# Tail-query scores as concurrent 64-row matmuls, with transposes and sums in one PSUM tile and smaller last output pieces

## The chip, the cores and the metric

The kernel runs on one core of a Trainium2 chip. The metric is the device time of one execution in microseconds (us). TensorE appears as PE in the profile, VectorE as DVE, ScalarE as ACT, GpSimd as POOL and SyncE as SP. The "granted clock" is the share of full TensorE clock that the throttle granted.

The spread of a single kernel is often 1% here. So two versions are compared only from runs of the same rounds on the same chip.

## The reference, cut to what matters

Attention with a relative position bias for 8 batches and 8 heads, then a bilinear feed-forward block on the result.

```python
# q, k, v: (8, 8, 576, 64); bias_table: (32, 8)
scores = q @ k.transpose(0, 1, 3, 2) / 8 + bias_table[bucket].transpose(2, 0, 1)[None]
attn = softmax(scores)                     # rows of 576 keys
x = (attn @ v).transpose(0, 2, 1, 3).reshape(4608, 512)
out = ((x @ w_a) * (x @ w_b)) @ w_out      # w_a, w_b: 512x1536, w_out: 1536x512
```

## The kernel before

Two heads form a head pair; there are 32 pairs, `p`, four to a batch. A sequence of 576 is cut into 512 "main" positions (four tiles of 128) and a "tail" of 64. Scores are made transposed, with keys on the partitions, so that the exponentials can be used as weights for `attn @ v`. The bias is a multiplication by `exp(bias)` after the exponential.

The schedule is written by hand. Stage `s` makes the scores of pair `s`, finishes pair `s-1` (its sums `av`, the normalisation into `XG`, the transposition into `xn`), and fills TensorE with units of the feed-forward block. A stage has two "score groups" (`qk(s, 0)` and `qk(s, 2)`). The first four pairs run in a denser prologue, and pairs 0 to 7 transpose Q and K on TensorE. From pair 8 on Q and K come transposed by DMA.

```python
ps_sc = ...tile_pool(name="ps_sc", bufs=2, space=PSUM)   # 2 tiles of 2 banks
ps_av = ...tile_pool(name="ps_av", bufs=1, space=PSUM)   # 1 bank: warm-up, av sums
ps_tr = ...tile_pool(name="ps_tr", bufs=1, space=PSUM)   # 1 bank: transposes
ps_ff = ...tile_pool(name="ps_ff", bufs=2, space=PSUM)   # 2 tiles of 1 bank
# ... (cut)
trb = ps_tr.tile([128, 1024], BF16, tag="tr", name="trb")

def tr_half():                       # the two halves of trb in turn
    turn[0] ^= 1
    return trb[:, 512 * turn[0]:512 * turn[0] + 512]

def qk(p, t0):                       # scores of main queries and main keys
    qT, kT, _ = operands(p)
    for t in (t0, t0 + 1):
        ps = ps_sc.tile([128, 2, 512], FP32, tag="sc", name=f"qk{p}_{t}")
        for hh in range(2):          # head hh lives on rows 64*hh..64*hh+63
            r = slice(64 * hh, 64 * hh + 64)
            nc.tensor.matmul(out=ps[:, hh, :], lhsT=kT[r, t, :], rhs=qT[r, :, :], ...)

def qk_tail(p):
    qT, kT, z = operands(p)          # z: both tails, block-diagonal (zeros elsewhere)
    ps = ps_sc.tile([128, 2, 512], FP32, tag="sc", name=f"qkt{p}")
    for t in range(NM):              # tail queries on main keys: 128 rows, 128 columns
        nc.tensor.matmul(out=ps[:, 0, :]...[:, :, t, :], lhsT=kT[:, t, :], rhs=z[:, 0, :], ...)
    # tail keys on main queries (512 columns), then on tail queries (2 x 64 columns)
    # ... (cut)

def mul_tail(p):                     # both multiplications by exp(bias) of a tail
    # ... (cut)
    nc.vector.tensor_tensor(out=x, in0=x, in1=e, op=MULT)                 # 128x512
    nc.vector.tensor_tensor(out=at[:, o:o + 192], ..., op=MULT)

def av(p, jqs, pool=None, tag="av"):
    pav = (pool or ps_av).tile([128, 3, 2, Dh + 1], FP32, tag=tag, ...)
    # ... (cut) matmuls into pav, then on DVE a reciprocal and a multiply for each
    # group, from pav into XG

def t_x(p, jqs=range(5), eng=None):  # XG -> xn
    if 4 <= p < NP - 1:
        nc.sync.dma_start_transpose(...)     # two transposing DMAs
        return
    ps = tr_half()                           # pairs 0-3 and 31: on TensorE
    # ... (cut) transposes, then a copy by ACT or DVE

def ff_o_last(c, tt, half):          # the last 128 rows of the output
    cs = slice(256 * half, 256 * half + 256)
    # ... (cut) 12 matmuls of 256 columns into po
    ob = wrk.tile([128, DM], FP32, tag="ob", ...)
    nc.scalar.activation(out=ob[:, 0:128], in_=po[:, 0:128], func=ACTF.Copy)
    nc.vector.tensor_copy(out=ob[:, 128:256], in_=po[:, 128:256])
    for hh, eng in enumerate((nc.sync, nc.scalar)):
        eng.dma_start(out=out[r0:r0 + ST, cs], in_=ob[64 * hh:64 * hh + 64, 0:256])

# prologue (cut to its middle)
av(1, h0, ps_ff, "ffn")
# ...
t_x(0, h0)
sc(1, 1)
av(2, h0)
mul_tail(0)
tail0(1)
t_x(1, h0)
# ...
# a stage; U stands for feed-forward units, A(...) for av of pair s-1
head = [U, ex(s, 1), A(0, 1, 2), U, mul(s, 0), t_q(s + 1), U, mul(s, 1)]
late = [A(3, 4), U, t_x(s - 1)]
pair = [v_next(s), (qk(s, 2), ex(s, 2)), U, ex(s, 3), t_k(s + 1, ACT), U, mul(s, 2)]
tail = [(qk_tail(s), ex_tail(s)), U, U, mul_tail(s)]
```

The softmax here doesn't subtract the row's maximum and nothing guards it: scores larger than these inputs give would overflow.

Of the kernel before, what the change touches and what calls it, by code (L numbers as in the profile page):

```python
# [13 lines left out]
def kernel(  # L14
# [35 lines left out]
    ps_sc = ctx.enter_context(tc.tile_pool(name="ps_sc", bufs=2, space=bass.MemoryType.PSUM))  # L50
    ps_av = ctx.enter_context(tc.tile_pool(name="ps_av", bufs=1, space=bass.MemoryType.PSUM))
    ps_tr = ctx.enter_context(tc.tile_pool(name="ps_tr", bufs=1, space=bass.MemoryType.PSUM))
    ps_ff = ctx.enter_context(tc.tile_pool(name="ps_ff", bufs=2, space=bass.MemoryType.PSUM))
# [57 lines left out]
    wo_sb = wpool.tile([128, NDF, DM], BF16, name="wo")  # L111
    xn_sb = [wpool.tile([128, NT], BF16, name=f"xn{mc}") for mc in range(NMC)]
    g_sb = [wpool.tile([128, DM], BF16, name=f"g{df}") for df in range(NDF)]

# [66 lines left out]
    def padding():  # L181
# [5 lines left out]
        for i in range(2):  # L187
# [14 lines left out]
                            op=mybir.AluOpType.subtract)  # L202
    warm = ps_av.tile([128, 512], FP32, tag="av", name="warm")

    def warm_up(n):
        for _ in range(n):
            nc.tensor.matmul(out=warm[:, :], lhsT=zero_sb[:, 0:128], rhs=zero_sb[:, :],
                             start=True, stop=True)
# [39 lines left out]

    trb = ps_tr.tile([128, 1024], BF16, tag="tr", name="trb")
    turn = [0]  # L250
# [70 lines left out]


    def qk(p, t0):
        qT, kT, _ = operands(p)
        st[p].setdefault("at", [None] * NM)
        for t in (t0, t0 + 1):
            ps = ps_sc.tile([128, 2, 512], FP32, tag="sc", name=f"qk{p}_{t}")
            for hh in range(2):
                r = slice(64 * hh, 64 * hh + 64)
                nc.tensor.matmul(out=ps[:, hh, :], lhsT=kT[r, t, :], rhs=qT[r, :, :],  # L330
                                 start=True, stop=True)
            st[p]["ps", t] = ps

    def ex(p, t):
# [45 lines left out]
    def qk_tail(p):  # L380
        qT, kT, z = operands(p)
        ps = ps_sc.tile([128, 2, 512], FP32, tag="sc", name=f"qkt{p}")
        for t in range(NM):
            nc.tensor.matmul(  # L384
                out=ps[:, 0, :].rearrange("p (h t c) -> p h t c", h=2, t=NM)[:, :, t, :],
                lhsT=kT[:, t, :], rhs=z[:, 0, :], start=True, stop=True)
# [13 lines left out]
    def ex_tail(p):  # L400
        ps, pt = st[p]["ps"]
        n = main_tail(p)
        at = att[p % 2]
        m = 512 + n
        if n < SM:
            m += ST
        else:
            nc.scalar.activation(out=at[:, m:m + ST], in_=pt, func=ACTF.Exp, scale=scale)
        nc.scalar.activation(out=at[:, 0:m], in_=ps[:, :, :].rearrange("p a x -> p (a x)")[:, 0:m],  # L409
                             func=ACTF.Exp, scale=scale)  # L410
        st[p]["att"] = at

    def mul_tail(p):
        at, w, wt = st[p]["att"], W_sb[p % 4], Wt_sb[:, p % 4, :]
        x = at[:, 0:512].rearrange("p (h t c) -> p h t c", h=2, t=NM)
# [3 lines left out]
        nc.vector.tensor_tensor(out=x, in0=x, in1=e, op=MULT)  # L419
        o = 512 + main_tail(p) - 128  # L420
        nc.vector.tensor_tensor(out=at[:, o:o + 192], in0=at[:, o:o + 192], in1=wt[:, 191::-1], op=MULT)

# [18 lines left out]
    def av(p, jqs, pool=None, tag="av"):  # L441
# [3 lines left out]
        rc = wrk.tile([128, 3, 2], FP32, tag="rc", name=f"rc{p}_{jqs[0]}")  # L445
        pav = (pool or ps_av).tile([128, 3, 2, Dh + 1], FP32, tag=tag, name=f"av{p}_{jqs[0]}")
        for slot, jq in enumerate(jqs):
# [64 lines left out]

    def ff_o_last(c, tt, half):
        cs = slice(256 * half, 256 * half + 256)
        po = ff_bank(f"po{c}_{tt}_{half}")
        for df in range(NDF):
            nc.tensor.matmul(out=po[:, 0:256], lhsT=g_sb[df][:, 128 * tt:128 * tt + 128],
                             rhs=wo_sb[:, df, cs], start=(df == 0), stop=(df == NDF - 1))
        ob = wrk.tile([128, DM], FP32, tag="ob", name=f"ob{c}_{tt}_{half}")
        nc.scalar.activation(out=ob[:, 0:128], in_=po[:, 0:128], func=ACTF.Copy)  # L520
        nc.vector.tensor_copy(out=ob[:, 128:256], in_=po[:, 128:256])
        for hh, eng in enumerate((nc.sync, nc.scalar)):
            r0 = S * (2 * tt + hh) + SM
            eng.dma_start(out=out[r0:r0 + ST, cs], in_=ob[64 * hh:64 * hh + 64, 0:256])

# [20 lines left out]
    for c in range(NCH):  # L546
# [8 lines left out]
        for tt in range(4):  # L555
            if c == NCH - 1 and tt == 3:
                units += [lambda c=c, tt=tt, half=half: ff_o_last(c, tt, half) for half in range(2)]
                continue
# [143 lines left out]
    for s in range(4, NP + 1):  # L702
# [12 lines left out]
        elif new:  # L715
            head = [U, lambda: ex(s, 1), A(0, 1, 2), U, lambda: mul(s, 0), lambda: t_q(s + 1), U,
                    lambda: mul(s, 1)]
            late = [A(3, 4), U, lambda: t_x(s - 1)]
            pair = [lambda: v_next(s), lambda: (qk(s, 2), ex(s, 2)), U, lambda: ex(s, 3),
                    lambda: t_k(s + 1, ACT), U, lambda: mul(s, 2)]  # L720
            tail = [lambda: (qk_tail(s), ex_tail(s)), U, U, lambda: mul_tail(s)]
# [63 lines left out]
```

## Time and profile before

| | before |
|---|---|
| median of 4 runs | 425.33 us (425.02 to 425.51) |
| span in the profile | 423.6 us |
| PE busy | 407.6 us, 96% |
| mean granted clock | 0.988 |

From the page of the kernel before: busy time of each engine with its share of the span (PE's line), then the busy tenths and the granted clock in 40 equal slices of the span, then the chain of work that ended last, by engine.

```profile
PE 407.6 (96%) x3471; PEld 207.6 (49%) x3471; DVE 239.0 (56%) x562; ACT 245.6 (58%) x347; POOL 130.7 (31%) x187
...
PE   7689899999999999999999999999999999999995
...
PEclk9689999999999999999999999999999999999999
...
PE 85%; DMA 7%; POOL 3%; DVE 2%; ACT 1%; issue 1%; ACTq 0%; DVEq 0%; POOLq 0%
```

PE is the bottleneck in nearly every slice. The exceptions are slices 1, 2, 3 and 5 (within the first 53 us) and the last one. So in the middle only matmul time counts, and at the two ends waits count.

The timeline of PE of the kernel before, in the prologue. Columns: start, duration, engine, line, operation, tiles (out<-in), row and column form, shape; a bracket gives idle time ahead and what ended it.

```profile
24.94 0.23 PE L448 MATMUL av<-vt,atk 128*128 128x130 bf16 x1
...
26.26 0.27 PE L480 MATMUL trb<-ident,XG 128*128 128x128 bf16 x2
26.37 0.22 PE L448 MATMUL av<-vt,atk 128*128 128x130 bf16 x1
...
28.37 0.27 PE L480 MATMUL trb<-ident,XG 128*128 128x128 bf16 x2
...
30.46 0.27 PE L480 MATMUL trb<-ident,XG 128*128 128x128 bf16 x2 [0.99 <-DVE xn L260]
...
31.33 0.22 PE L448 MATMUL av<-vt,att 128*128 128x130 bf16 x1
...
35.10 0.23 PE L448 MATMUL av<-vt,att 128*128 128x130 bf16 x1
...
36.06 0.33 PE L480 MATMUL trb<-ident,XG 128*128 128x128 bf16 x3
```

Transposes (into `trb`) and sums (into `av`) follow one another almost without idle time. They lie in different tiles. The one wait shown, at 30.46, is of transposes for a copy out of their own tile `trb`.

The waits of PE from 20 to 100 us, kernel before: waiting line, what it waited for, total us, times, longest. Then the busy times of the engines from 24 to 50 us (PE, PEld, DVE, ACT, POOL, then granted clock, DMA share, GB/s).

```profile
PE trb L480 <- DVE xn L260: 1.0, 1, 1.0
PE pa L498 <- DMA kn<-in_k_dram: 0.9, 1, 0.9
...
PE av L448 <- DVE XG L462: 0.2, 1, 0.2
```

```profile
24.00:50.00 26.00, 23.27 (x329) 16.64 (x326) 21.52 (x66) 18.33 (x29) 14.31 (x20) 0.99 1.39 189
```

A tail in the steady part, from PE's timeline of the kernel before: four matmuls of tail queries on main keys, one of 512 columns, two of 64. It lasts from 210.89 to 211.39 (the start of the next matmul), that is 0.50 us. The last two lines are feed-forward matmuls.

```profile
210.89 0.39 PE L384 MATMUL qkt<-ZB,KB 128*128 128x128 bf16 x4
211.12 0.38 PE L388 MATMUL qkt<-QB,ZB 128*128 128x512 bf16 x1
211.33 0.22 PE L392 MATMUL trb<-ZB 128*128 128x64 bf16 x2
...
244.79 1.03 PE L498 MATMUL pa<-xn,wa 128*128 128x512 bf16 x4
245.65 1.03 PE L508 MATMUL pb<-xn,wb 128*128 128x512 bf16 x4
```

The end, from the timeline of all engines of the kernel before. The last matmul ends at 418.65.

```profile
419.70 0.28 ACT L520 ACTIVATE ob<-po 128x128 f32<-128x128 f32 x1 [1.49 <-DMA out_dram<-ob]
420.01 0.29 DVE L521 COPY ob<-po 128x128 f32<-128x128 f32 x1 [1.47 <-ACT ob L520]
420.34 0.50 ACTq L524 DMA_DIRECT2D out_dram<-ob  x1
```

The last copy of ACT waits for an older output DMA out of the same buffer, then DVE's copy waits for ACT's, then come issue and landing.

### The profile page before, as it was taken

What the parts mean: (1) busy time and instruction counts of PE and PEld (TensorE: products, weight loads), DVE (VectorE), ACT (ScalarE), POOL (GpSimd) and SP (SyncE); (2) the same over time, 40 slices, a digit from 0 to 9 for tenths busy, and PEclk for the clock granted to TensorE, in tenths of its full rate; (3) what the DMA queues carried; (4) which work ended last, traced back from release to release, by engine and by line L of the source; (5) the groups of instructions that cost most, each with busy time, mean ns of one, the idle gap of its engine ahead of it and who ended that gap; (6) DMA issues with size and microseconds to landing.
All of it is one profiled execution on the core that took longest, in us unless ns stands there. A gap on an engine that the chain in (4) does not pass through costs nothing.

```text
span 423.6 us, 8798 instructions
## 1 busy us (share of the span) xinstructions
PE 407.6 (96%) x3471; PEld 207.6 (49%) x3471; DVE 239.0 (56%) x562; ACT 245.6 (58%) x347; POOL 130.7 (31%) x187
## 2 busy tenths in 40 slices
PE   7689899999999999999999999999999999999995
PEld 3367545535555444555454544454545455444443
DVE  5788568546654776467646665476547662431320
ACT  4676676566665766576657674866566742322321
POOL 9654458596008700690039201500000000000000
PEclk9689999999999999999999999999999999999999
DMA  9999999999439970999099905950430012002004
GB/s 117 200 201 171 204 144 187 140 185 130 82 73 148 124 106 19 151 159 119 16 128 158 139 15 115 143 90 17 88 91 15 15 39 76 1 2 99 0 8 94
DMA packets 139756, 42.46 MB, mean 100 GB/s; under 512 B 115994, under 2 KB 135226, under 8 KB 139714
## 3 DMA queue, kind: packets, MB, share of 16 engines
q0 software_dynamic: 81264, 18.89, 57.5%
q1 hardware_dynamic: 53010, 13.67, 20.4%
q10 hardware_dynamic: 5440, 9.34, 7.1%
q8 instruction: 27, 0.44, 0.5%
q14 instruction: 15, 0.12, 0.1%
HBM read 39.18 MB, written 9.45 MB: 115 GB/s over the span
## 4 chain that ended last, share of the span: by engine, by line
PE 85%; DMA 7%; POOL 3%; DVE 2%; ACT 1%; issue 1%; ACTq 0%; DVEq 0%; POOLq 0%
PE pb L508 22%; PE pa L498 22%; PE po L531 21%; PE av L452 9%; PE qk L330 7%; DMA kn<-in_k_dram 4%; PE av L448 2%; DMA wb<-in_moe_w_b_dram 2%; PE qkt L384 1%; PE qkt L388 1%; POOL qn L121 1%; POOL vt L159 1%; POOL kn L121 1%; POOL tl L153 1%; DMA out_dram<-ob 1%
## 5 line engine op out<-in xcount | busy, mean ns | idle before, releaser
L337 ACT ACTIVATE at<-qk 128x1024 bf16<-128x1024 f32 x112 | 111.5, 1024 | 29.1 <-PE qk L330 11.1
L511 DVE TENSOR_TENSOR g<-pb,ha 128x512 bf16<-128x512 f32 (+1 forms) x112 | 75.1, 671 | 79.4 <-PE pb L508 61.5
L498 PE MATMUL pa<-xn,wa 128*128 128x512 bf16 (+1 forms) x448 | 112.1, 372 | 1.8 <-DMA kn<-in_k_dram 0.9
L508 PE MATMUL pb<-xn,wb 128*128 128x512 bf16 (+1 forms) x448 | 111.8, 372 | 0.1
L502 ACT ACTIVATE ha<-pa 128x512 f32<-128x512 f32 (+1 forms) x112 | 65.2, 582 | 73.5 <-PE pa L498 73.5
L531 PE MATMUL po<-wo,g 128*128 128x512 bf16 x420 | 99.1, 379 | 0.0
L342 DVE TENSOR_TENSOR at<-at,W 128x1024 bf16<-128x1024 bf16 x112 | 75.0, 684 | 20.5 <-ACT at L337 20.5
L498 PEld LDWEIGHTS <-wa 128*128 128x128 bf16 x448 | 40.2, 98 | 48.0 <-issue 8.3
L508 PEld LDWEIGHTS <-wb 128*128 128x128 bf16 x448 | 39.6, 98 | 46.3 <-issue 9.7
L531 PEld LDWEIGHTS <-g 128*128 128x128 bf16 x420 | 38.0, 98 | 44.8 <-issue 5.3
L159 POOL DMA_DIRECT2D vt<-in_v_dram x16 | 10.9, 698 | 112.4 <-PE av L452 112.2
L461 DVE RECIPROCAL rc<-av 128x6 f32<-128x6 f32 (+3 forms) x96 | 16.4, 171 | 47.4 <-PE av L452 45.7
L535 ACT ACTIVATE ob<-po 128x512 f32<-128x512 f32 x35 | 20.9, 598 | 36.6 <-PE po L531 30.5
L452 PE MATMUL av<-vm,at 128*128 128x65 bf16 x896 | 41.2, 194 | 0.2 <-DVE vm L318 0.2
L452 PEld LDWEIGHTS <-at 128*128 128x128 bf16 x896 | 37.2, 98 | 6.6 <-issue 0.3
L130 POOL DMA_DIRECT2D qn<-in_q_dram x48 | 36.2, 795 | 8.0 <-DMA wo<-in_moe_w_out_dram 6.7
L462 DVE TENSOR_TENSOR XG<-av,rc 128x384 bf16<-128x384 f32 (+3 forms) x96 | 36.2, 377 | 3.5 <-DVE rc L461 0.2
L139 POOL DMA_DIRECT2D kn<-in_k_dram x48 | 36.1, 781 | 4.5 <-PE pa L498 2.7
L448 PE MATMUL av<-vt,att 128*128 128x130 bf16 x152 | 33.3, 219 | 0.2 <-DVE XG L462 0.2
L409 ACT ACTIVATE att<-qkt 128x1024 bf16<-128x1024 f32 (+1 forms) x32 | 32.1, 1002 | 1.1 <-PE qkt L392 1.1
L330 PE MATMUL qk<-QB,KB 64*128 64x512 bf16 x192 | 29.4, 381 | 0.1
L419 DVE TENSOR_TENSOR att<-att,W 128x512 bf16<-128x512 bf16 x32 | 13.5, 422 | 11.2 <-ACT att L409 11.2
(81 smaller groups left out, 281.3 us busy)
## 6 DMA issues: line engine op xcount, KB each, us to landing
out_dram<-ob ACTq DMA_DIRECT2D x32, 256.0 KB, 3.2
vn<-in_v_dram POOLq DMA_DIRECT2D x16, 256.0 KB, 6.0
kn<-in_k_dram POOLq DMA_DIRECT2D x48, 64.0 KB, 4.9
qn<-in_q_dram POOLq DMA_DIRECT2D x48, 64.0 KB, 4.0
wa<-in_moe_w_a_dram POOLq DMA_DIRECT2D x3, 512.0 KB, 9.4
wb<-in_moe_w_b_dram POOLq DMA_DIRECT2D x3, 512.0 KB, 12.0
wo<-in_moe_w_out_dram POOLq DMA_DIRECT2D x1, 1536.0 KB, 16.2
qn<-in_q_dram POOLq DMA_DIRECT2D x8, 128.0 KB, 6.2
```

The source lines that it names most:

```text
L130: nc.gpsimd.dma_start(out=by_tile(qn[b % 2])[:, h0 // 4, t, :, :], in_=q[b, h0:h1, 128 * t:128 * t + 128, :].transpose([1, 0, 2]))
L330: nc.tensor.matmul(out=ps[:, hh, :], lhsT=kT[r, t, :], rhs=qT[r, :, :], start=True, stop=True)
L337: nc.scalar.activation(out=at[:, :, :], in_=ps[:, :, :], func=ACTF.Exp, scale=scale)
L342: nc.vector.tensor_tensor(out=at[:, :, :], in0=at[:, :, :], in1=w[:, :, S - 1 + t:S - 1 + t - SM:-1], op=MULT)
L448: nc.tensor.matmul(out=pav[:, slot, :, :], lhsT=weights_tail(p, jq), rhs=vt[i][:, hp, :, :], start=True, stop=True)
L452: nc.tensor.matmul(out=pav[:, slot, hh, :], lhsT=weights(p, t, hh, jq), rhs=vm[i][:, 2 * hp + hh, t, :], start=False, stop=True, skip_grou ...
L462: nc.vector.tensor_tensor(out=xg[0:np_, j0:j0 + n, :, :], in0=pav[0:np_, s0:s0 + n, :, 0:Dh], in1=r.unsqueeze(3).to_broadcast([np_, n, 2, ...
L498: nc.tensor.matmul(out=pa[:, 0:n], lhsT=wa_sb[df // 4][:, mc, 128 * (df % 4):128 * (df % 4) + 128], rhs=xn_sb[mc][:, 512 * c + lo:512 * c ...
L502: nc.scalar.activation(out=ha[:, 0:n], in_=pa[:, 0:n], func=ACTF.Copy)
L508: nc.tensor.matmul(out=pb[:, 0:n], lhsT=wb_sb[df // 4][:, mc, 128 * (df % 4):128 * (df % 4) + 128], rhs=xn_sb[mc][:, 512 * c + lo:512 * c ...
L511: nc.vector.tensor_tensor(out=g_sb[df][:, lo:lo + n], in0=pb[:, 0:n], in1=ff["ha"][:, 0:n], op=MULT)
L531: nc.tensor.matmul(out=po[:, :], lhsT=g_sb[df][:, 128 * tt:128 * tt + 128], rhs=wo_sb[:, df, :], start=(df == 0), stop=(df == NDF - 1))
```

## The change

The intent: in `qk_tail` half of every 128-row contraction multiplies zeros. Two 64-row matmuls in the two row halves of the array can run at the same time: the two of a score group start 3 ns apart (206.264 and 206.267 in the kernel before). So these scores are to be made in pairs of 64-row matmuls. They go into the second score group, which already is in 64-row form. Heads 0 and 1 are given a PSUM bank each, as in the other scores, and no bank is free: the pools already take eight (4 + 1 + 1 + 2), which is all there are by the Trainium skill, "PSUM — Partial Sum Buffer", Specifications (TRN2). So the transposes' bank and the sums' bank become one tile `ab` of two banks, shared by three uses. Separately, the last 512 output columns are made in pieces of 256, 128 and 128 from an own buffer.

```diff
-    ps_av = ctx.enter_context(tc.tile_pool(name="ps_av", bufs=1, space=bass.MemoryType.PSUM))
-    ps_tr = ctx.enter_context(tc.tile_pool(name="ps_tr", bufs=1, space=bass.MemoryType.PSUM))
+    ps_ab = ctx.enter_context(tc.tile_pool(name="ps_ab", bufs=1, space=bass.MemoryType.PSUM))
...
-    warm = ps_av.tile([128, 512], FP32, tag="av", name="warm")
+    ab = ps_ab.tile([128, 2, 512], FP32, tag="ab", name="ab")
+    warm = ab[:, 1, :]
...
-    trb = ps_tr.tile([128, 1024], BF16, tag="tr", name="trb")
+    trb = ab[:, 0, :].bitcast(BF16)
...                                            (in qk, for pairs from 8 on)
+        if shared(p) and t0 == 2:
+            z = operands(p)[2]
+            for t in range(NM):
+                for hh in range(2):
+                    r = slice(64 * hh, 64 * hh + 64)
+                    nc.tensor.matmul(out=ab[:, hh, ST * t:ST * t + ST], lhsT=kT[r, t, :],
+                                     rhs=z[r, 0, ST * hh:ST * hh + ST], start=True, stop=True)
+    def ex_rows(p):
+        nc.scalar.activation(out=at[:, 0:512]..., in_=ab[:, :, 0:256], func=ACTF.Exp, scale=scale)
...                                            (qk_tail keeps 512 + 2 x 64 columns)
     def mul_tail(p):
+        if not shared(p):
+            mul_rows(p)                        (the 128x512 multiply, else put elsewhere)
...                                            (in av)
-        pav = (pool or ps_av).tile([128, 3, 2, Dh + 1], FP32, tag=tag, ...)
+        if pool:
+            pav = pool.tile([128, 3, 2, Dh + 1], FP32, tag=tag, ...)
+        else:
+            pav = ab[:, 1, 0:6 * (Dh + 1)].rearrange("p (j h d) -> p j h d", j=3, h=2)
...                                            (the last columns)
-        ob = wrk.tile([128, DM], FP32, tag="ob", name=f"ob{c}_{tt}_{half}")
-        nc.scalar.activation(out=ob[:, 0:128], in_=po[:, 0:128], func=ACTF.Copy)
-        nc.vector.tensor_copy(out=ob[:, 128:256], in_=po[:, 128:256])
+        copy(nc.vector if c0 else nc.scalar, ob_last[:, c0:c0 + n], po[:, 0:n])
...                                            (the stage)
+            if shared(s):
+                pair = [lambda: v_next(s), lambda: (qk(s, 2), ex(s, 2), ex_rows(s)), U,
+                        lambda: ex(s, 3), U, lambda: mul(s, 2), lambda: mul_rows(s)]
```

More of the change, by code (lines that the diff above doesn't have):

```diff
@@ L112 @@
     xn_sb = [wpool.tile([128, NT], BF16, name=f"xn{mc}") for mc in range(NMC)]
+    ob_last = wpool.tile([128, DM], FP32, name="ob_last")
     g_sb = [wpool.tile([128, DM], BF16, name=f"g{df}") for df in range(NDF)]
@@ L202 @@
                             op=mybir.AluOpType.subtract)
-    warm = ps_av.tile([128, 512], FP32, tag="av", name="warm")
+    ab = ps_ab.tile([128, 2, 512], FP32, tag="ab", name="ab")
+    warm = ab[:, 1, :]
     def warm_up(n):
         for _ in range(n):
-            nc.tensor.matmul(out=warm[:, :], lhsT=zero_sb[:, 0:128], rhs=zero_sb[:, :],
+            nc.tensor.matmul(out=warm, lhsT=zero_sb[:, 0:128], rhs=zero_sb[:, :],
                              start=True, stop=True)
@@ L320, in v_in, with shared @@
             in_=vn[b % 2][:, 256 * h0:256 * h1].rearrange("p (h t d) -> p h t d", t=NM, d=Dh))
+    def shared(p):
+        return p >= 8
     def qk(p, t0):
@@ L332, in qk @@
             st[p]["ps", t] = ps
+        if shared(p) and t0 == 2:
[6 more added lines that the diff above has]
+    def ex_rows(p):
+        st[p]["att"] = at = att[p % 2]
+        nc.scalar.activation(out=at[:, 0:512].rearrange("p (h x) -> p h x", h=2), in_=ab[:, :, 0:256],
+                             func=ACTF.Exp, scale=scale)
     def ex(p, t):
@@ L382, in qk_tail @@
         ps = ps_sc.tile([128, 2, 512], FP32, tag="sc", name=f"qkt{p}")
+        if shared(p):
+            nc.tensor.matmul(out=ps[:, 0, :], lhsT=z[:, 1, :], rhs=qT[:, :, :], start=True, stop=True)
+            for hh in range(2):
+                nc.tensor.matmul(out=ps[:, 1, 0:ST], lhsT=z[:, 1, :], rhs=z[:, 0, ST * hh:ST * hh + ST],
+                                 start=(hh == 0), stop=(hh == 1))
+            st[p]["ps"] = (ps, None)
+            return
         for t in range(NM):
@@ L404, in ex_tail @@
         m = 512 + n
+        st[p]["att"] = at
+        if shared(p):
+            nc.scalar.activation(out=at[:, 512:m + ST],
+                                 in_=ps[:, :, :].rearrange("p a x -> p (a x)")[:, 0:SM + ST],
+                                 func=ACTF.Exp, scale=scale)
+            return
         if n < SM:
@@ L410, in ex_tail, with mul_rows @@
                              func=ACTF.Exp, scale=scale)
-        st[p]["att"] = at
     def mul_tail(p):
-        at, w, wt = st[p]["att"], W_sb[p % 4], Wt_sb[:, p % 4, :]
+        if not shared(p):
+            mul_rows(p)
+        at, wt = st[p]["att"], Wt_sb[:, p % 4, :]
+        o = 512 + main_tail(p) - 128
+        nc.vector.tensor_tensor(out=at[:, o:o + 192], in0=at[:, o:o + 192], in1=wt[:, 191::-1], op=MULT)
+    def mul_rows(p):
+        at, w = st[p]["att"], W_sb[p % 4]
         x = at[:, 0:512].rearrange("p (h t c) -> p h t c", h=2, t=NM)
@@ L419, in mul_tail @@
         nc.vector.tensor_tensor(out=x, in0=x, in1=e, op=MULT)
-        o = 512 + main_tail(p) - 128
-        nc.vector.tensor_tensor(out=at[:, o:o + 192], in0=at[:, o:o + 192], in1=wt[:, 191::-1], op=MULT)
     def weights(p, t, hh, jq):
@@ L445, in av @@
         rc = wrk.tile([128, 3, 2], FP32, tag="rc", name=f"rc{p}_{jqs[0]}")
-        pav = (pool or ps_av).tile([128, 3, 2, Dh + 1], FP32, tag=tag, name=f"av{p}_{jqs[0]}")
+        if pool:
+            pav = pool.tile([128, 3, 2, Dh + 1], FP32, tag=tag, name=f"av{p}_{jqs[0]}")
+        else:
+            pav = ab[:, 1, 0:6 * (Dh + 1)].rearrange("p (j h d) -> p j h d", j=3, h=2)
         for slot, jq in enumerate(jqs):
@@ L511, in ff_b, with ff_o_last @@
         nc.vector.tensor_tensor(out=g_sb[df][:, lo:lo + n], in0=pb[:, 0:n], in1=ff["ha"][:, 0:n], op=MULT)
-    def ff_o_last(c, tt, half):
-        cs = slice(256 * half, 256 * half + 256)
-        po = ff_bank(f"po{c}_{tt}_{half}")
+    def ff_o_last(c, tt, c0, n):
+        po = ff_bank(f"po{c}_{tt}_{c0}")
         for df in range(NDF):
-            nc.tensor.matmul(out=po[:, 0:256], lhsT=g_sb[df][:, 128 * tt:128 * tt + 128],
-                             rhs=wo_sb[:, df, cs], start=(df == 0), stop=(df == NDF - 1))
-        ob = wrk.tile([128, DM], FP32, tag="ob", name=f"ob{c}_{tt}_{half}")
-        nc.scalar.activation(out=ob[:, 0:128], in_=po[:, 0:128], func=ACTF.Copy)
-        nc.vector.tensor_copy(out=ob[:, 128:256], in_=po[:, 128:256])
+            nc.tensor.matmul(out=po[:, 0:n], lhsT=g_sb[df][:, 128 * tt:128 * tt + 128],
+                             rhs=wo_sb[:, df, c0:c0 + n], start=(df == 0), stop=(df == NDF - 1))
+        copy(nc.vector if c0 else nc.scalar, ob_last[:, c0:c0 + n], po[:, 0:n])
         for hh, eng in enumerate((nc.sync, nc.scalar)):
             r0 = S * (2 * tt + hh) + SM
-            eng.dma_start(out=out[r0:r0 + ST, cs], in_=ob[64 * hh:64 * hh + 64, 0:256])
+            eng.dma_start(out=out[r0:r0 + ST, c0:c0 + n], in_=ob_last[64 * hh:64 * hh + 64, c0:c0 + n])
     def ff_o(c, tt, part):
@@ L556 @@
             if c == NCH - 1 and tt == 3:
-                units += [lambda c=c, tt=tt, half=half: ff_o_last(c, tt, half) for half in range(2)]
+                units += [lambda c=c, tt=tt, c0=c0, n=n: ff_o_last(c, tt, c0, n)
+                          for c0, n in ((0, 256), (256, 128), (384, 128))]
                 continue
@@ L718 @@
             late = [A(3, 4), U, lambda: t_x(s - 1)]
-            pair = [lambda: v_next(s), lambda: (qk(s, 2), ex(s, 2)), U, lambda: ex(s, 3),
-                    lambda: t_k(s + 1, ACT), U, lambda: mul(s, 2)]
+            if shared(s):
+                pair = [lambda: v_next(s), lambda: (qk(s, 2), ex(s, 2), ex_rows(s)), U,
+                        lambda: ex(s, 3), U, lambda: mul(s, 2), lambda: mul_rows(s)]
+            else:
+                pair = [lambda: v_next(s), lambda: (qk(s, 2), ex(s, 2)), U, lambda: ex(s, 3),
+                        lambda: t_k(s + 1, ACT), U, lambda: mul(s, 2)]
             tail = [lambda: (qk_tail(s), ex_tail(s)), U, U, lambda: mul_tail(s)]
```

## The prediction

> **What bounds the kernel now.** TensorE. The page's first table has PE busy 407.6 of 423.6 us, the chain of waits puts 85% on PE, and the table by stretches shows PE busy 45.00 of 45.00 us in most stretches from 95 to 320 us, at clock 1.00. There only matmul time counts. In the timeline from 24 to 50 us PE, ACT and DVE take turns and PE is in small waits. At the very end a serial tail (copy, issue, landing) counts.
>
> **Gain 1, matmuls.** A tail now takes 0.50 us of PE (timeline, 210.89 to 211.39): four 128-column matmuls 56 ns apart (0.223 us), one of 512, two of 64. The first four go. In their place come four pairs of 64-row, 64-column matmuls inside a score group that is in 64-row form already, so no further change of form (about 92 ns each now) is paid. The Trainium skill, "TensorE: Matmul & The Clock Gate", Part 3, says that matmuls in different row groups run concurrently; the trace agrees, the two score matmuls of a pair start 3 ns apart. I estimate 32 ns a pair, the pitch of the 65-column av matmuls: 0.13 us. Net 0.09 us for 24 head pairs: -2.2 us, all on the critical path. ACT work hardly changes (512 + 576 columns for 1024 + 64).
>
> New waits there: the new scores wait for the normalisation of the first av group, which ends 1.37 us before they would be through; the second av group waits for the new exp, which I place 0.3 us before it. No stall, but a thin margin.
>
> **Gain 2, last columns.** The last ACT copy waits for an older output DMA (419.60), then ACT 0.28 and DVE 0.29 us run in series, issue at 420.34. With its own buffer and one DVE copy of 128 columns the last issue comes about 419.0: -1.3 us.
>
> **Loss.** Transposes and av sums now share one tile, `ab`. The listing of each engine's instructions with the instruction each waits for shows waits by the whole tile: a transpose into bank 0 now waits for the last DVE read of av in bank 1, and an av matmul for the last copy out of the transposes. For head pairs 0 to 7 (to 80 us) both are used in turn. Laid on the trace: av(2) waits for the xn copy ending 26.20, not 24.94; then four times a transpose waits for reciprocal/multiply/reciprocal/multiply (1.05 us after the av), and twice an av waits for an ACT copy queued behind an exp (0.8 to 1.2 us). Following PE, ACT and DVE by hand to 50 us, I get about 6 us. Stages 5 and 6 add 0.3 each. PE is full afterwards, so nothing gives it back but some 0.5 us of waits around 91 us. At the end of attention the last pair's transposes wait for its last multiply: +1.1 us (350.84 to 351.9).
>
> **Sum.** 425.3 + 6 + 0.6 - 0.5 + 1.1 - 2.2 - 1.3 = about 429 us; hand serialisation overstates, so **428.4 us**, 80% range **424.8 to 431.5**. Faster by over 2%: 0.01; within: 0.95; slower: 0.04.
>
> **What would show it.** PE idle between 24 and 50 us up by some 5 us, ended by DVE XG, DVE xn/QT copies, ACT xn/KT copies; first matmul of pair 8 later by 5 to 6 us; a four-stage period of 44.5 us shorter by 0.36; new pairs about 32 ns apart; one PE gap near 352 us; last issue 1.3 us closer to the last matmul.
>
> **What would make it wrong.** The start hides more of the waits (then near 424); new pairs at 60 ns; the second av group stalling in 18 stages; a lower granted clock.

## The result

| | before | after |
|---|---|---|
| median of 4 runs | 425.33 us (425.02 to 425.51) | 437.48 us (435.10 to 438.93) |
| ratio | | 1.0281 (1.0235 to 1.0327), slower |
| span in the profile | 423.6 us | 435.8 us |
| PE busy | 407.6 us | 407.3 us |
| mean granted clock | 0.988 | 0.975 |

A ratio is the mean time of one kernel's fast runs over the mean of the other's fast runs of the same rounds, so it is not quite the ratio of the medians quoted. The bracket is a 95% interval. Executions over 1.5% slower than the fastest of the same kernel are left out of the means.

The page of the kernel after, the same lines:

```profile
PE 407.3 (93%) x3518; PEld 211.4 (49%) x3579; DVE 237.9 (55%) x562; ACT 244.3 (56%) x346; POOL 130.3 (30%) x187
...
PE   6677799899999999999999999999999999999996
...
PEclk9666999999999999999999999999999999999999
...
PE 82%; DVE 9%; issue 4%; ACT 3%; DMA 1%; POOL 0%; DVEq 0%; ACTq 0%; POOLq 0%
```

The loss is in the first five slices: PE is less busy in slices 1, 3, 4 and 5, and the clock is lower in slices 3 and 4. DVE is now 9% of the chain, against 2%.

PE's timeline of the kernel after, in the prologue:

```profile
27.43 0.22 PE L484 MATMUL ab<-vt,atk 128*128 128x130 bf16 x1 [1.69 <-DVE xn L261]
...
33.51 0.27 PE L516 MATMUL ab<-ident,XG 128*128 128x128 bf16 x2 [1.12 <-DVE XG L498]
...
37.34 0.27 PE L484 MATMUL ab<-vt,att 128*128 128x130 bf16 x1 [1.07 <-ACT xn L259]
...
44.02 0.22 PE L484 MATMUL ab<-vt,att 128*128 128x130 bf16 x1 [1.16 <-ACT KT L259]
...
46.31 0.33 PE L516 MATMUL ab<-ident,XG 128*128 128x128 bf16 x3 [1.19 <-DVE XG L498]
...
363.61 0.33 PE L516 MATMUL ab<-ident,XG 128*128 128x128 bf16 x3 [0.97 <-DVE XG L498]
```

The matmul at 27.43 writes sums in bank 1 but waits for a copy out of the transposes in bank 0. The transposes at 33.51 write bank 0 but wait until DVE has read the sums in bank 1. None of these waits was there in the kernel before; the counterparts of the first five lines are those at 24.94, 28.37, 31.33, 35.10 and 36.06 above. The last line is the same wait at the end of attention (in the kernel before, these transposes start at 350.84 without one). PE's waits from 20 to 100 us and the busy times from 24 to 50 us, kernel after:

```profile
PE ab L516 <- DVE XG L498: 2.6, 3, 1.2
PE ab L484 <- ACT KT L259: 2.5, 3, 1.2
PE ab L484 <- DVE xn L261: 1.8, 2, 1.7
PE ab L269 <- DVE XG L498: 1.1, 1, 1.1
PE ab L484 <- ACT xn L259: 1.1, 1, 1.1
```

```profile
24.00:50.00 26.00, 18.81 (x241) 13.68 (x239) 16.42 (x50) 12.78 (x19) 15.28 (x21) 0.78 1.37 196
```

These five waits on `ab` are 9.1 us in sum. From 24 to 50 us the granted clock is 0.78 against 0.99.

The new matmuls and the rest of a tail, PE's timeline of the kernel after:

```profile
206.47 0.61 PE L334 MATMUL qk<-QB,KB 64*128 64x512 bf16 x4
206.91 0.28 PE L342 MATMUL ab<-ZB,KB 64*128 64x64 bf16 x8
...
255.76 0.38 PE L400 MATMUL qkt<-QB,ZB 128*128 128x512 bf16 x1
255.97 0.22 PE L402 MATMUL qkt<-ZB 128*128 128x64 bf16 x2
256.03 1.03 PE L534 MATMUL pa<-xn,wa 128*128 128x512 bf16 x4
257.35 1.02 PE L544 MATMUL pb<-xn,wb 128*128 128x512 bf16 x4 [0.29 <-DVE g L547]
```

The members of a pair start 3 ns apart (206.910 and 206.913), the pairs 28 to 29 ns apart. A score group takes 0.655 us instead of 0.537, a tail 0.273 instead of 0.497. That is 0.106 us a pair gained, a little over the 0.09 predicted. But the last line shows a wait of 0.29 us that the kernel before hadn't. From the start of the `pa` matmuls ahead of it to the `pb` matmuls it takes 1.32 us, against 0.86 in the kernel before (244.79 to 245.65).

The end, all engines, kernel after (last matmul ends at 431.45):

```profile
429.47 1.12 ACTq L575 DMA_DIRECT2D out_dram<-ob  x2
430.64 0.38 ACT L259 ACTIVATE ob_last<-po 128x256 f32<-128x256 f32 x1 [1.20 <-PE po L552]
431.05 1.80 ACTq L557 DMA_DIRECT2D out_dram<-ob_last  x3
431.49 0.29 DVE L261 COPY ob_last<-po 128x128 f32<-128x128 f32 x1 [0.38 <-PE po L552]
```

ACT issues the output of the previous rows until 430.59 and only then copies. Six issues of 0.5 to 0.8 us each on two queues follow, and the last one ends at 433.13, 1.35 us after the last copy. Before, the last issue began 0.03 us after the last copy and ended 0.53 us after it.

Where the 12.2 us of span went, from the start of every pair's first score matmul in both traces. The pairs' starts are at 79.98 and 92.88 (pair 8), 123.95 and 135.70 (pair 12), 335.64 and 347.38 (pair 31):

| stretch | predicted | measured in the traces |
|---|---|---|
| start to pair 8 | +6.0 and +0.6 | +12.9 |
| pairs 8 to 12 | -0.5 given back, and part of -2.2 | -1.2 |
| pairs 12 to 31 | the rest of -2.2 | 0.0 |
| last transposes | +1.1 | +1.1 |
| from last matmul to end | -1.3 | -0.6 (4.95 to 4.36) |
| sum | +3.7, trimmed to +3.1 | +12.2 |

The +12.9 has three parts. The first `av` begins at 21.62 instead of 20.66 (+1.0). From there to pair 8 PE is idle for 11.0 us instead of 3.0 (+8.1). The remaining 3.9 us are matmuls that took longer, and that is the clock: in this stretch PE's matmuls were under way at half clock for 12.1 us instead of 4.1, and half of the difference is 4.0. The clock was at one half for 10.2 us of the first 25 us in both kernels, and in the kernel after again from 28.41 to 31.82 and 35.23 to 42.06.

### The profile page after: what moved, and what is told of

It reads as the page before. It is cut to its first block, busy times and chain, and to the rows that moved or that the text cites. A ratio compares the mean times of both kernels' runs of the same rounds, so it can differ in the third digit from the quotient of the medians.

```text
span 435.8 us, 8958 instructions
## 1 busy us (share of the span) xinstructions
PE 407.3 (93%) x3518; PEld 211.4 (49%) x3579; DVE 237.9 (55%) x562; ACT 244.3 (56%) x346; POOL 130.3 (30%) x187
## 4 chain that ended last, share of the span: by engine, by line
PE 82%; DVE 9%; issue 4%; ACT 3%; DMA 1%; POOL 0%; DVEq 0%; ACTq 0%; POOLq 0%
PE po L564 20%; PE pb L544 20%; PE pa L534 19%; PE ab L488 9%; PE qk L334 6%; PE ab L484 2%; DVE g L547 2%; DVE at L358 2%; DVE XG L498 1%; PE qkh L369 1%; DMA kn<-in_k_dram 1%; DVE ath L384 1%; PE qkt L400 1%; DVE rc L497 1%; ACT at L353 1%
## 5 line engine op out<-in xcount | busy, mean ns | idle before, releaser
L353 ACT ACTIVATE at<-qk 128x1024 bf16<-128x1024 f32 x112 | 113.4, 1027 | 34.3 <-PE qk L334 16.1
L564 PE MATMUL po<-wo,g 128*128 128x512 bf16 x399 | 97.6, 379 | 1.2 <-issue 0.2
L544 PEld LDWEIGHTS <-wb 128*128 128x128 bf16 x448 | 39.7, 98 | 44.2 <-issue 7.6
L497 DVE RECIPROCAL rc<-ab 128x6 f32<-128x6 f32 (+3 forms) x94 | 16.0, 170 | 61.9 <-PE ab L488 61.8
L488 PE MATMUL ab<-vm,at 128*128 128x65 bf16 x896 | 41.2, 194 | 0.2 <-DVE vm L319 0.2
L484 PE MATMUL ab<-vt,att 128*128 128x130 bf16 x152 | 33.6, 221 | 3.7 <-ACT KT L259 2.5
L498 DVE TENSOR_TENSOR XG<-ab,rc 128x384 bf16<-128x384 f32 (+3 forms) x94 | 35.3, 376 | 3.2
L430 ACT ACTIVATE att<-qkt 128x576 bf16<-128x576 f32 x24 | 15.6, 649 | 13.5 <-PE qkt L402 13.5
L375 ACT ACTIVATE ath<-qkh 128x1024 bf16<-128x1024 f32 x16 | 15.7, 1022 | 10.4 <-PE qkh L369 10.4
## 6 DMA issues: line engine op xcount, KB each, us to landing
wb<-in_moe_w_b_dram POOLq DMA_DIRECT2D x3, 512.0 KB, 10.1
```

The lines of the kernel that those rows point to most:

```text
L353: nc.scalar.activation(out=at[:, :, :], in_=ps[:, :, :], func=ACTF.Exp, scale=scale)
L484: nc.tensor.matmul(out=pav[:, slot, :, :], lhsT=weights_tail(p, jq), rhs=vt[i][:, hp, :, :], start=True, stop=True)
L488: nc.tensor.matmul(out=pav[:, slot, hh, :], lhsT=weights(p, t, hh, jq), rhs=vm[i][:, 2 * hp + hh, t, :], start=False, stop=True, skip_grou ...
L498: nc.vector.tensor_tensor(out=xg[0:np_, j0:j0 + n, :, :], in0=pav[0:np_, s0:s0 + n, :, 0:Dh], in1=r.unsqueeze(3).to_broadcast([np_, n, 2, ...
L544: nc.tensor.matmul(out=pb[:, 0:n], lhsT=wb_sb[df // 4][:, mc, 128 * (df % 4):128 * (df % 4) + 128], rhs=xn_sb[mc][:, 512 * c + lo:512 * c ...
L564: nc.tensor.matmul(out=po[:, :], lhsT=g_sb[df][:, 128 * tt:128 * tt + 128], rhs=wo_sb[:, df, :], start=(df == 0), stop=(df == NDF - 1))
```

## The experiments

The theory after the result: (T1) the shared tile is the whole loss, by waits and by the lower clock that those waits bring; (T2) the clock is an extra cause that can be taken away without the waits; (T3) the early multiply of tail scores eats the gain of the new matmuls. The rivals: (R1) the new matmuls themselves cost more than they gain; (R2) the last columns cost; (R3) the lower clock is a state of the chip and has nothing to do with the change. Every run gave a correct result.

### The shared tile alone

The kernel before, with the one tile `ab` and nothing else of the change.

```diff
-    ps_av = ...;  ps_tr = ...
+    ps_ab = ...
+    ab = ps_ab.tile([128, 2, 512], FP32, tag="ab", name="ab")
+    warm = ab[:, 1, :];  trb = ab[:, 0, :].bitcast(BF16);  pav = ab[:, 1, 0:6 * (Dh + 1)]...
```

> The kernel before, with nothing changed but that transposes and av sums sit in one tile of two banks. If the loss comes from waits by the whole tile (theory 1), this alone is slower than the changed kernel's 437.5 us minus what the rest of the change gains: about 438 to 441 us, with granted clock 0.5 in part of 25 to 50 us and pair 8 starting near 92 us. If the loss comes from the new score matmuls or the new exp (rival), this stays at 425 to 427 us.

Measured: 436.68 us (434.18 to 438.66), ratio 1.0253 (1.0191 to 1.0315), span 436.4, clock 0.974. The waits of PE from 20 to 100 us in this kernel:

```profile
PE ab L483 <- DVE XG L465: 2.6, 3, 1.2
PE ab L451 <- ACT KT L258: 2.3, 3, 1.2
PE ab L451 <- DVE xn L260: 1.9, 2, 1.6
```

These three are those of the kernel after, each within 0.2 us. Pair 8 starts 13.24 us later than before (12.91 in the kernel after). So the shared tile alone makes the whole loss within the noise, and R1 and R2 are not needed for it. The time is under the 438 to 441 us that I expected, because I still credited the rest of the change with a gain that it didn't bring: at pair 31 the two traces are 11.72 and 11.74 us late.

### Shared only where it is needed

The change, but with the two old tiles up to pair 7 and `ab` from stage 8 on, in the banks that they leave.

```diff
+    first = ExitStack()
+    ps_av = first.enter_context(...);  ps_tr = first.enter_context(...)
...
+        if s == 8:
+            first.close()
+            ps_ab = ...;  ab = ps_ab.tile([128, 2, 512], FP32, tag="ab", name="ab")
...                           (the last pair's transposes use a ps_ff tile)
```

> The whole change, but transposes and av sums keep tiles of their own until pair 7 is done, the shared tile is made at pair 8, and the last pair's transposes go to a bank of the output matmuls. Theory 1: no loss at the start, pair 8 starts at 80 us as before; what is left is the gain: 1.2 us from the periodic part and 0.6 us from the last columns, so 423 to 424 us. Rival: stays over 433 us.

Measured: 428.17 us (424.93 to 429.49), ratio 1.0045 (0.9986 to 1.0104), span 425.5. The start is repaired: pair 8 begins at 77.79, 2.2 us before the kernel before. The 2.2 us are probably luck and not the edit's, since up to there the two kernels do the same work in tiles of their own: this trace has full clock throughout the start, where that of the kernel before had 10.2 us at half. The time missed what I expected by over 4 us. PE's timeline of this kernel shows why:

```profile
91.97 0.59 PE L538 MATMUL pa<-xn,wa 128*128 128x512 bf16 x1 [3.51 <-DMA xn<-XG]
```

The transposing DMAs of pair 7 were issued at 82.99 and 84.31 and landed at 91.93 and 93.11. The kernel before issued them at 85.39 and 87.16, and they landed at 91.72 and 93.33. So coming earlier gained nothing: PE just waited there, and ran at half clock from 89.98 to 96.80. Together that cost 4.9 us from pair 9's first to its second score group. At best such a transpose lands 2.3 us after its issue began, later in the same traces; here it took 8.9 and 8.8 us. (The kernel before waits 0.89 us at the same place. The profile puts that down to a load of K, but the first transpose landed at 91.72, just before PE went on at 91.77, so it is probably the same wait.)

### The last columns alone

```diff
(the kernel before, with ob_last and the pieces of 256, 128, 128 only)
```

> The kernel before with only the last output columns in pieces of 256, 128, 128 from a buffer of their own. The traces put the end of the last matmul to the end of the span at 4.95 us before and 4.36 us after, so 0.6 us faster: 424.7 us. If the prediction's 1.3 us were right in a quieter start, 424.0 us.

Measured: 425.58 us (424.30 to 425.84), ratio 0.9985 (0.9937 to 1.0034), span 424.1. No loss (R2 falls), and no gain that the rounds can resolve. In its trace the end takes 4.98 us, no less than the 4.95 before: the issues stand as in the kernel after, but the last output lands 0.6 us later after its issue. (Eight other traces with these pieces have 4.34 to 4.36, one 3.98.) As in the kernel after, the two queues hold three issues each, so the queueing is the pieces' own.

### The multiply at its old place

```diff
     def mul_tail(p):
-        if not shared(p):
-            mul_rows(p)
+        mul_rows(p)
...
-                        lambda: ex(s, 3), U, lambda: mul(s, 2), lambda: mul_rows(s)]
+                        lambda: ex(s, 3), U, lambda: mul(s, 2)]
```

> The changed kernel, with the multiply of the tail-query scores put back to the end of the stage, where it was before. In the trace a pb matmul waits 0.29 us for a late DVE multiply once in four stages; if that comes from the earlier multiply, the four-stage period falls from 44.53 to about 44.2 us and the time by 6 times 0.3, 1.8 us, to 435.7 us. If it comes from the order of ACT instead, the period stays and the time too.

Measured: 436.59 us (434.85 to 437.11), ratio 1.0247 (1.0202 to 1.0292), span 435.1. Its shift against the kernel before is 12.75 us at pair 12, 12.20 at 16, 11.88 at 20, 11.57 at 24 and 11.26 at 28. So from pair 16 on it gains about 0.31 us every four stages, where the kernel after gained nothing (11.75, 11.54, 11.56, 11.59, 11.61). The period fell to the 44.2 us expected, and T3 holds by the traces. The time did not fall to the 435.7 us expected: this run had 17.1 us at half clock between 25 and 60 us, against 10.2 in the trace of the kernel after. It was run at another time. In the kernel after the early multiply of 128x512 stands on DVE ahead of the normalisation and of the product `g`:

```profile
254.88 0.42 DVE L454 TENSOR_TENSOR att<-att,W 128x512 bf16<-128x512 bf16 x1
...
256.61 0.68 DVE L547 TENSOR_TENSOR g<-pb,ha 128x512 bf16<-128x512 f32 x1
```

Once in four stages a matmul of the feed-forward block then waits 0.29 us for `g`. Stage by stage the sum closes: three of four stages are 0.11 us shorter than before, and the fourth (11.48 us against 11.13) gives that back. With the late multiply the fourth is as long as before.

### The two together, and pair 7 transposed on TensorE

First, the split tiles with the late multiply:

> Tiles apart until pair 7, and the tail-score multiply back at the end of the stage. Theory: the early multiply costs 0.34 us in four stages, so the period falls from 44.54 us to about 44.1 (0.11 us for each of four stages under the 44.51 of before), and stages 12 to 31 save about 2 us against before. The whole time also depends on a wait for a transposing DMA near 92 us, which the split kernel's trace shows 3.5 us long: if that stays, about 426; without it 423.

Measured: 423.97 us (422.31 to 425.02), ratio 0.9973 (0.9924 to 1.0022), span 421.7. From pair 12 to 31 its shift goes from +0.11 to -1.23, less than the 2 us expected. The wait for the transposing DMA is 1.0 us in this trace, whose pair 8 began at 80.41 and not at 77.79.

Second, the same with pair 7 not transposed by DMA:

```diff
-        if 4 <= p < NP - 1:
+        if 4 <= p < NP - 1 and p != 7:
             nc.sync.dma_start_transpose(...)
...
+            if s == 8:
+                steps += head + [A(3, 4), U, U, lambda: (t_x(7, (0, 1, 2)), t_x(7, (3, 4)))] + pair
```

> As the last one, but the output of pair 7 is transposed by TensorE in stage 8 and not by DMA. If the 3.5 us wait near 92 us is the DMA transposes of pair 7 standing in a full DMA queue, it goes, and with it the spell of half clock after it: 2 to 4 us less than the last one, near 422. If PE waits there for loads of the next batch instead, the wait stays under another name and the time is the same.

Measured: 420.60 us (420.06 to 422.38), ratio 0.9905 (0.9858 to 0.9951), span 418.3. The wait near 92 us is gone from its timeline. So the DMA transposes of pair 7 were the thing waited for. The means of the two kernels' four runs are 2.9 us apart. The two profiled runs alone do not show what the wait costs: 2.4 us of their 3.4 lie before pair 8, where the kernels do not differ and the first of them had 6.8 us at half clock, the second none.

### The waits left, the clock held up

The kernel after, with matmuls on zeros into a feed-forward bank ahead of six of the waits (5 or 4 matmuls of 512 columns each), so that PE is busy where it would be idle. Nothing that makes it wait is taken away.

```diff
+    def fill(n):
+        f = ps_ff.tile([128, 512], FP32, tag="ffn", name="fill")
+        for _ in range(n):
+            nc.tensor.matmul(out=f[:, :], lhsT=zero_sb[:, 0:128], rhs=zero_sb[:, :], ...)
...
+    fill(5)                # ahead of av(2, h0); fill(4) ahead of five more
     av(2, h0)
```

> The changed kernel with 25 filler matmuls of zeros, four or five in front of each of the six longest new waits at the start. They do no useful work. If the half clock between 28 and 42 us comes from the gaps and costs some 3.5 us, the clock stays at 1.00 there and the time falls from 437.5 to about 434 although PE does more. If the fall of the clock is not from the gaps, or costs nothing, the time stays at 437.5 or rises.

Measured: 433.74 us (432.62 to 435.32), ratio 1.0208 (1.0148 to 1.0268), span 432.2, clock 0.997. Busy times of this kernel from 24 to 50 us:

```profile
24.00:50.00 26.00, 21.83 (x289) 14.19 (x286) 17.87 (x56) 12.31 (x19) 14.94 (x21) 1.00 1.35 200
```

The granted clock is 1.00, against 0.78 in the kernel after, although useless work was added. That speaks for T2 and against R3, and all 14 traces say the same: between 25 and 60 us the clock was at half for 10.2 to 17.1 us in the four with the shared tile from the start and no fillers, and never in the other ten. But the kernel after had not run in this call. So both were run again in one call, in five rounds.

> The changed kernel unaltered, on the same chip as the fillers, since the first comparison was across two calls and its intervals overlap. 437 us, granted clock under 0.985 in most runs.

> The changed kernel with the 25 fillers, on the same chip. If the low clock costs what the traces say, 3.5 us less than the kernel without fillers, and a granted clock of 0.994 or more in most runs; if the first result was luck, the same time.

Measured: the kernel after again 435.02 us (433.99 to 439.27), ratio 1.0233 (1.0179 to 1.0287); with the fillers 432.88 us (432.74 to 433.97), ratio 1.0180 (1.0139 to 1.0221). The means are 436.07 and 433.19, so the fillers bring 2.9 us (by the scatter of the runs, 0.4 to 5.4 us with 95%), a little under the 3.5 expected. The kernel after was 2.5 us faster here by the median than in its first call, and only three of its six runs had a clock under 0.985, where I had expected most. These six runs also sort by their clock:

| granted clock of the run | time, us |
|---|---|
| 0.976, 0.977 | 439.27, 438.85 |
| 0.984 | 435.73 |
| 0.991, 0.992, 0.992 | 434.30, 433.99, 434.27 |

The six filler runs have clocks of 0.993 to 1.000 and lie within 1.3 us. So in this call the scatter of the changed kernel goes with the clock: 1 to 6 us against the fillers' mean. In its first call it did not: the runs of 435.10, 437.34 and 438.93 us had 0.987, 0.988 and 0.987, so part of the scatter is unexplained. The other 7.7 us of the loss (433.19 against 425.52, the mean of the kernel before) are there with the clock held up: the waits.

### The same scores in 128-row form

The split version with the eight new matmuls of 64 columns in 128-row form, as the zeros in `z` allow. The loads, banks and positions stay the same.

```diff
-                    nc.tensor.matmul(out=ab[:, hh, ...], lhsT=kT[r, t, :], rhs=z[r, 0, ...])
+                    nc.tensor.matmul(out=ab[:, hh, ...], lhsT=kT[:, t, :], rhs=z[:, 0, ...])
```

> Tiles apart until pair 7; the eight new score matmuls of a stage use all 128 rows, half of them zeros, in place of 64. Same columns, same banks, same place. If 64-row matmuls in two row groups run at the same time, the eight take about 0.25 us here against 0.12 us, and the gap to the next matmul group grows by about 0.13 us in each of 24 stages (3 us over stages 8 to 31). If the saving comes from the move alone, the stage is as long as with 64 rows.

Measured: one run, 431.38 us, span 429.6. It is a single run, so the time is not used; the trace is:

```profile
199.79 0.61 PE L336 MATMUL qk<-QB,KB 64*128 64x512 bf16 x4
200.32 0.41 PE L343 MATMUL ab<-ZB,KB 128*128 128x64 bf16 x8
```

In the trace the eight matmuls now stand 29 ns apart one after the other (but for the first step, 38 ns), and the group takes 0.780 us instead of 0.655. Against the split version each stage from 10 to 30 is 0.11 to 0.12 us longer (2.4 us in sum). Stage 9 is 0.56 us longer, but there the wait for pair 7 is longer too (4.6 us). So it is the running side by side that gains, as the Trainium skill says in "TensorE: Matmul & The Clock Gate", Part 3, for different row groups; the split version's trace agrees, with 3 to 4 ns between the members of a pair. That is most of R1; the rest, the net gain, is measured in the next section. The same trace shows the cost of changing between 64-row and 128-row form: 308 ns from the last 64-row score matmul's start to the next matmul, where 216 ns is the step without a change. That is 92 ns. The Trainium skill, "TensorEngine Tiling (Array Packing)", Key Properties, says that a change of mode drains TensorE, and gives no figure.

### The best version, and how much of it is the change

The version with pair 7 on TensorE and the last columns in two pieces of 320 and 192, both copied by DVE. And the kernel before with only these last two edits, so without the 64-row scores.

```diff
-        copy(nc.vector if c0 else nc.scalar, ob_last[:, c0:c0 + n], po[:, 0:n])
+        copy(nc.vector, ob_last[:, c0:c0 + n], po[:, 0:n])
...
-                          for c0, n in ((0, 256), (256, 128), (384, 128))]
+                          for c0, n in ((0, 320), (320, 192))]
```

> All that worked together: tiles apart until pair 7, tail-score multiply at the end of the stage, pair 7 transposed by TensorE, and the last columns in two pieces of 320 and 192, both copied by DVE so that ACT's queue only issues. The end from the last matmul should shrink from 4.95 us (before) and 4.36 us (the change) to about 3.7 us: 420 us, some 1.3% under before and a little under the version without the last step (420.6).

> The control: the kernel before, with the tail scores as they were, but with the transposes of pair 7 on TensorE and the two last pieces of 320 and 192. If the 64-row score pairs are worth their place, this is slower than the last one by about 24 times 0.1 us, 2 to 2.5 us: near 422.5 us. If they are worth nothing, the two are equal.

Measured: the best version 420.39 us (420.00 to 421.27), ratio 0.9868 (0.9827 to 0.9908). The kernel before with the two side edits 422.95 us (421.86 to 424.16), ratio 0.9928 (0.9885 to 0.9970). So the best version beats both kernels, by 1.3% and, by the two ratios to the kernel before, about 4%, and of its gain the 64-row scores and what goes with them bring 2.5 us. (One run of the kernel before, 430.30 us, lies just under the limit for a slow run and is counted; without it the gain is 1.2%.) From the last matmul's end to the end of the span it takes 3.69 us, against 4.95 before and 4.36 after. That is the 1.3 us that I had promised for the last columns: it takes four issues instead of the six of the kernel after, and no copy on the engine that is issuing.

### The clock and the busy share

All 14 traces record when the granted clock changed. The stretches at half clock last 3.41, 6.83 or 10.24 us (but for the last of each trace, which runs past the end of the span). That fits the window of 4096 cycles (3413 ns) which the Trainium skill gives in "TensorE: Matmul & The Clock Gate", Part 1, "What's actually happening". I cut the first 110 us and the end of every trace into such windows and took PE's busy share of each:

| clock in the window | clock after it | PE's busy share of the window |
|---|---|---|
| full | fell to half | up to 0.56 |
| full | stayed full | from 0.42, in most windows 0.57 or more |
| half | rose to full | 0.89 or more |
| half | stayed half | up to 0.82 |

The two upper rows overlap between 0.42 and 0.56, and the phase of the windows is not known for certain, so this is a tendency and no threshold. The page's closing table, "Why this matters for your kernels", says to allow no idle gaps over about 3 us. In the kernel after no gap later than 13 us was longer than 1.69 us, and the clock fell all the same at 21.58, 28.41 and 35.23: short gaps in one window had left PE busy for about half of it (0.53, 0.51 and 0.52).

## Why the prediction was wrong

It said 428.4 us and at most 431.5; it was 437.5. "Within 2%" had 0.95, and it was slower by 2.8%. The mechanism was the right one: waits by the whole tile. The step that failed is the sum. It gave the lower clock no size, and that was the largest error (3.9 us); stage 6, the first `av` and the two gains were mis-sized too. Predicted before the trim was +3.7 us, measured in the profiles +12.2.

1. **"The listing ... shows waits by the whole tile"**: right. The waits, their places and what ended them are as predicted: a wait for the `xn` copy at 27.43, then for XG and for ACT's copies. The shared tile alone brought 1.0253.
2. **"Following PE, ACT and DVE by hand to 50 us, I get about 6 us"**, with 0.6 us for stages 5 and 6, then trimmed with "hand serialisation overstates": the replay itself was right. PE's idle time from the first `av` to pair 5 (48 us in the kernel before) rose by 6.3 us. After that it rose by 0.3 us in stage 5, 1.3 in stage 6, where I had put 0.3, and 0.2 in stage 7, so by 8.1 us to pair 8. The replay did not overstate, and I cut the sum by 0.6 us for it. The first `av` came 1.0 us later, which I hadn't looked at: the warm-up matmuls share the tile too, and in all six traces with the shared tile from the start they wait for it (in the kernel after three times, at 8.57, 12.58 and 15.91), in no other trace. How much of the 1.0 us is theirs is not settled, since the first `av` also varies among kernels with tiles of their own (18.9 to 20.9 us, against 21.1 to 21.6 with the shared tile).
3. **"What would make it wrong: ... a lower granted clock"**: the term that failed most. It was named and then counted as nothing, in the sum and in the range. It cost 3.9 us in the profiled run, and 2.9 us on average by the experiment with fillers. Since the waits make the clock fall, the term belonged in the sum.
4. **"Net 0.09 us for 24 head pairs: -2.2 us, all on the critical path"** and **"No stall, but a thin margin"**: the first of them right as far as the matmuls go, the second not. The matmuls gain 0.106 us a pair. But I had looked at the margins of PE and ACT alone and not at DVE's order, where the tail's multiply had moved forward. That put a wait of 0.29 us, 0.45 us between the starts of matmuls, into one of four stages, which is what four stages gain, and from pair 12 to 31 the net gain was 0.0. With the multiply at its old place 0.31 us per four stages came back.
5. **"-1.3 us" for the last columns**: half of it, -0.6, and nothing in the trace of the last columns alone. The copy no longer waited for an old DMA, but six issues queued up on two engines, and the first copy stood behind issues on ACT.
6. **"+1.1 us" for the last transposes**: right, +1.06 with 0.97 us of wait.
7. **"Nothing gives it back but some 0.5 us of waits around 91 us"**: it was 1.2 us, because the late kernel comes to this place in a quiet stretch: it issued the second transpose of pair 7 at 91.74, and it landed at 94.12. The other side was seen only in the versions that come earlier and find the transposes not landed: the split version waits 3.5 us there and loses the clock.

Still open are three things. The fillers take PE time themselves and may have delayed some useful work, so their 2.9 us may understate what the clock cost. Why the transposes of pair 7 land so late was not settled. The traces point to other DMA traffic. In five traces whose DMA share (of the view by stretches) from 83 to 92 us is 1.4 to 2.3 (the kernel before: 2.01) they land 6.1 to 10.1 us after the issue, between 91.7 and 95.4. In the six with 0.1 to 0.4 (all with the shared tile from the start, which issue them 1 to 6 us later) the one of the two whose landing is recorded takes 2.4 us, and lands as early as 90.3 in those with fillers. But no run changed that traffic alone. And why the compiler's bookkeeping tracks the two banks of `ab` as one, while it lets pieces of the buffer `ob_last` pass each other, was not looked into.

## What to carry to other kernels

When two buffers with different rhythms are merged into one tile, look at every stretch in which both are used in turn, not only at the one the change is made for; if only the later part needs the merger, give the banks over at that point. Waits of 1 us that come close together can cost twice, because the TensorE clock may fall with the busy share: put the clock into the sum of a prediction once PE falls near half busy for some microseconds. A gain on the bottleneck engine arrives only if nothing else on the way is late, so follow the order on the idle engines (here DVE) and the next arrival that does not come earlier with it (here the DMA transposes near 92 us) before booking it.

## What the Trainium skill lacked or had wrong

- "TensorE: Matmul & The Clock Gate", Part 1 and the closing table: the table's rule is for single gaps over about 3 us; Part 1 also tells of a kernel whose frequent short idles made the clock swing, but gives no busy share for it. In the kernel after, later than 13 us, gaps of at most 1.69 us were enough where they left PE busy for 0.51 to 0.53 of a window. Over all traces the clock fell after windows of up to 0.56, rose again only after windows of 0.89 or more, and stayed low at up to 0.82.
- "TensorEngine Tiling (Array Packing)", Key Properties: a change of mode drains, without a figure. Measured: 92 ns a change (308 against 216 ns).
- The same page and "TensorE: Matmul & The Clock Gate", Part 3: no figure for short concurrent matmuls. Measured: pairs of 64-row, 64-column matmuls stand 28 to 29 ns apart, the same as single 128-row matmuls of 64 columns (29 ns), so at half the time for the same work.
- "DMA: Bandwidth & Descriptors", "Latency and other measured facts": a bandwidth for transposing DMAs, but nothing on their landing under load. Measured from the start of the issue, for those of pair 7: 2.4 us with little other traffic (DMA share 0.1 to 0.4 from 83 to 92 us), 6.1 to 10.1 us with much (1.4 to 2.3); and each of the last output issues holds its queue for 0.5 to 0.8 us.
- No page: that two banks allocated as one tile are waited for as one. Measured: 9.1 us of waits on `ab` from 20 to 100 us.
